# Transposing the adapter input by DMA instead of by TensorE and VectorE, in an attention kernel followed by a mixture of adapters

## The chip, the core and the metric

The kernel runs on one core of a Trainium2 chip. Five engines work side by side, each with its own instruction order: TensorE (PE in the profile, its weight loads PEld), VectorE (DVE), ScalarE (ACT), GpSimd (POOL) and SyncE (SP), which here only issues DMAs. An engine runs its instructions in the order in which the program gives them, and an instruction may wait for semaphores that other engines or DMAs raise. The metric is device time in microseconds of one execution, the median of several runs; the profile describes one further execution.

## The reference, cut to what matters

```python
scores = scale * q @ k.T + bias          # 8 batches, 8 heads, 576 positions, head size 64
attn   = softmax(scores) ; y = attn @ v  # bias from a table of 32 buckets, by distance
x = y.transpose(0, 2, 1, 3).reshape(8 * 576, 512)

logits = x @ w_gate                      # 8 adapters, the 2 best of each row
w = softmax(logits of the 2 best)
out = x + sum over them of w * ((x @ A[e]) @ B[e])   # A: 512 x 16, B: 16 x 512 each
```

Inputs and output are fp32; the kernel computes the matrix products in bf16.

## The kernel before

**Units and slots.** The attention is cut into 32 units: a unit `u` is one batch and one pair of heads (`hp`, 0 to 3), in the order `units` = (0,0), (0,1) ... (7,3). The main loop has six slots per unit. Each slot computes a part of the unit's scores on PE, exponentials on ACT (L260, L268), the bias products on DVE (L285, L274), and, for the unit before, the products with v (`values`, L303). In slot 5 `normalise` (L313, L314) writes the unit before into `xn`, the rows of x in bf16. A batch's rows are four tiles of 128 and 64 rows over; the spare rows of two batches share the tile `xe`, one half of which is moved by a DMA (L320).

**Loads.** `load(b)` makes a list of 28 DMAs for batch b, by head pairs: q, k and v of a pair (128 KB each head), with the last 64 positions after the first pair (`qke32`, `ve32`). The list is put on the SP queue, up to three DMAs a slot in units 0 and 1 and one or two later. Batch 0 and 1 are loaded at the start; batch b + 2 is put on the queue from slot 4 of the third unit of batch b. The staging buffers hold two batches. POOL casts q, k and v to bf16 two units and one unit ahead (`cast_qk`, `cast_v`, L129, L133), and the spare rows before the next batch (`cast_tails`). PE transposes q and k of a unit (`transpose_pe`, L224), DVE copies them out of PSUM (L228).

**SP's order.** All loads, the moves to `xe` and all stores of the output (L409) stand in one SP queue, in program order. A DMA there that has to wait holds up those behind it. The program uses eight completion semaphores for SP's DMAs in turn, so that each issue also waits for the eighth before it.

**Adapters.** A, w_gate and B are loaded by six DMAs of POOL in unit 3 (`load_adapters`, L204 to L209), which cast to bf16 on the way. Finished tiles of x are taken in groups of two or three by `Group`. Its steps: transposes of x on PE (`xT_pe`, L342) and the copy out of PSUM on DVE (`xT_out`, L347); the product with A and w_gate together (`zl_pe`, L355); the copy to SBUF on ACT (`z_copy`) and the choice of the two best (`gates`, DVE, POOL and ACT); the weights (`weigh`); the transpose of the weighted z (`zT_pe`, `zT_out`); and per tile the product with B (`dl_pe`, L403), the sum with x on DVE (`dl_out`, L407) and the store (L409). A step is a pair, a PE part and a DVE part. `batch_done` calls `enqueue`, one group after even batches and two after odd ones, and this puts the steps on a list, mixed with the last steps of the group before. `place` takes one step from the list in slots 0, 2 and 4 of a unit (in the last two batches in slot 5 too): the PE part goes into the next slot, the DVE part is done at the next `place`. The first group (three tiles of batch 0) has its `zl_pe` at the end of unit 5. The last batch's own rows are done by `Last` after the main loop, with transposes on PE; nothing in it changes.

Of the kernel before, what the change touches and what calls it, by code (L numbers as in the profile page):

```python
# [11 lines left out]
FP32 = mybir.dt.float32  # L12
BF16 = mybir.dt.bfloat16
# [20 lines left out]
def kernel(  # L34
# [34 lines left out]
    cp = ctx.enter_context(tc.tile_pool(name="const", bufs=1))  # L69
# [19 lines left out]
    def load(b):  # L89

        q32 = stg.tile([128, 4, H, D], FP32, name="q32", tag="q32")
        k32 = stg.tile([128, 4, H, D], FP32, name="k32", tag="k32")
        v32 = stg.tile([128, 4, H, D], FP32, name="v32", tag="v32")
        qke32 = stg.tile([128, H, D], FP32, name="qke32", tag="qke32")
        ve32 = stg.tile([128, HP, D], FP32, name="ve32", tag="ve32")
        staged[b] = (q32, k32, v32, qke32, ve32)
        todo = []

        def main(eng, t, src, hp):
            for h in (2 * hp, 2 * hp + 1):  # L100
                todo.append(lambda h=h: eng.dma_start(  # L101
                    out=t[:, :, h, :],
                    in_=src[b, h, :512, :].rearrange("(j p) d -> p j d", p=128)))

        for hp in range(HP):
            second = nc.scalar if b == 0 and hp == 0 else nc.sync
            main(nc.sync, q32, q, hp)
            main(second, k32, k, hp)
# [5 lines left out]
            main(nc.sync, v32, v, hp)  # L114
# [26 lines left out]
    units = [(b, hp) for b in range(B) for hp in range(HP)]  # L141
# [57 lines left out]
    AW = cp.tile([128, 4, ER + E], BF16, tag="AW")  # L199
    Bc = cp.tile([ER, Dm], BF16, tag="Bc")  # L200

    def load_adapters(c):
        if c < 4:
            nc.gpsimd.dma_start(out=AW[:, c, :ER].rearrange("p (e r) -> p e r", e=E),  # L204
                                in_=moe_A[:, c * 128:(c + 1) * 128, :].rearrange("e d r -> d e r"))
        elif c == 4:
            nc.gpsimd.dma_start(out=AW[:, :, ER:], in_=moe_w_gate.rearrange("(c p) e -> p c e", p=128))
        else:
            nc.gpsimd.dma_start(out=Bc, in_=moe_B.rearrange("e r d -> (e r) d"))  # L209


    xs, xe, probs, accs = {}, {}, {}, {}
# [94 lines left out]
    def normalise(u):  # L307
        b, hp = units[u]
        pv = accs.pop(u)
        if hp == 0:  # L310
            xs[b] = xp.tile([128, 5, Dm], BF16, name="xn", tag="xn")
        rc = ms.tile([128, 2, 5], FP32, name="rc", tag="rc")
        nc.vector.reciprocal(rc, _ap(pv, D, [[512, 2], [W, 5]]))  # L313
        nc.vector.tensor_tensor(  # L314
            _ap(xs[b], hp * 128, [[D, 2], [Dm, 5], [1, D]]),
            _ap(pv, 0, [[512, 2], [W, 5], [1, D]]),
            _ap(rc, 0, [[5, 2], [1, 5], [0, D]]), op=ALU.mult)
        if hp == HP - 1 and b % 2 == 0:
            xe[b // 2] = xp.tile([128, Dm], BF16, name="xe", tag="xe", bufs=2)
            nc.sync.dma_start(out=xe[b // 2][:64, :], in_=xs[b][64:, 4, :])  # L320
        if hp == HP - 1 and b % 2 and b + 1 < B:
            join(b, 0, Dm)

    def join(b, c0, c1):
        nc.vector.tensor_copy(xe[b // 2][64:, c0:c1], xs[b][64:, 4, c0:c1])


    queue = deque()
    state = {"now": None, "last": None}

    class Group:
# [3 lines left out]
            self.n = len(tiles)  # L335
            self.xT = []

        def xT_pe(self, t0, n):
            self.ps = mp.tile([128, n, 4, 128], BF16, name="xT_ps", tag="mm")
            for t in range(n):  # L340
                for c in range(4):
                    nc.tensor.transpose(self.ps[:, t, c, :],  # L342
                                        self.x[t0 + t][:, c * 128:(c + 1) * 128], ident)

        def xT_out(self, n):
            xT = ms.tile([128, n, 4, 128], BF16, name="xT", tag=f"xT{n}")
            nc.vector.tensor_copy(xT, self.ps)  # L347
            self.xT += [xT[:, t] for t in range(n)]

        def zl_pe(self, t0, n):  # L350
            if t0 == 0:
                self.zl = mp.tile([128, self.n, ER + E], FP32, name="zl", tag="mm")
            for t in range(t0, t0 + n):
                for c in range(4):
                    nc.tensor.matmul(self.zl[:, t, :], lhsT=self.xT[t][:, c, :], rhs=AW[:, c, :],  # L355
                                     start=(c == 0), stop=(c == 3), skip_group_check=True)
# [54 lines left out]
        def front(self):  # L411
            n2 = min(self.n, 2)
            s = [(lambda: self.xT_pe(0, n2), lambda: self.xT_out(n2))]
            if self.n == 3:
                s.append((lambda: self.xT_pe(2, 1), lambda: self.xT_out(1)))
                s.append((lambda: (self.zl_pe(0, 3), self.z_copy()), self.gates))
            else:
                s.append((lambda: (self.zl_pe(0, n2), self.z_copy()), self.gates))
            return s

        def middle(self):
            return [(self.zT_pe, self.zT_out)]

        def back(self):
            return [(lambda t=t: self.dl_pe(t), lambda t=t: self.dl_out(t))
                    for t in range(self.n)]
# [6 lines left out]
    def enqueue(tiles):  # L433
        gr, last = Group([tile_of(*t) for t in tiles]), state["last"]
        front, fill = gr.front(), last.back() if last else []
        fill += [(None, None)] * (2 - len(fill))
        pe, dve = fill[1]
        fill[1] = (pe, lambda: (dve and dve(), gr.weigh()))
        queue.extend(front[:1] + (last.middle() if last else []) + front[1:] + fill)
        state["last"] = gr  # L440

    def flush():
        if state["last"]:
            queue.extend(state["last"].middle() + state["last"].back())
            state["last"] = None

    due = {}

    def at(slot, fn, *args):
        due.setdefault(slot, []).append((fn, args))  # L450
# [16 lines left out]

    def batch_done(b):
        if b % 2 == 0:
            if b + 2 < B:  # L470
                enqueue([(b, 0), (b, 1), (b, 2)])
                left.append((b, 3))
            else:
                enqueue([(b, 0), (b, 1)])
                enqueue([(b, 2), (b, 3)])
# [105 lines left out]
    def finish(p, t):  # L581
        normalise(p)
        if units[p][1] == HP - 1:
            at(t + 1, batch_done, units[p][0])

    for t in range(SLOTS * NU):
        u, s = divmod(t, SLOTS)
        b, hp = units[u]
        p = u - 1
        scores(u, s)  # L590
        for fn, args in due.pop(t, []):
            fn(*args)
        if u == 3:
            load_adapters(s)
        for i in range(3 if u < 2 else 2 if s % 3 == 0 else 1):
            if loading:
                loading.popleft()()
        early = u >= NU - HP and hp in (0, HP - 1)
# [63 lines left out]
    u = NU - 1  # L662
# [6 lines left out]
    last = Last(B - 1)  # L669
# [43 lines left out]
```

## Time and profile before

| What | Value |
|---|---|
| median of 3 runs | 231.32 us (231.14 to 232.71) |
| the profiled execution | 233.92 us; its span, from the first to the last instruction, 231.8 us |
| TensorE clock granted, mean over the span | 0.955 |
| DMA moved | 39.74 MB in 126521 packets, 120464 of them under 512 bytes |
| the loads' queue | 68.2% of 16 engines' span; POOL's queue 3.5% |
| a load of 128 KB, from issue to landing | 2.9 to 3.1 us (median) |
| start of `xn` (L314) of units 3, 7, 15, 23, 31 | 41.09, 62.66, 114.77, 165.38, 216.99 us |

The busy share of an engine is the mean over stages with different limits. The chain of waits follows the execution back from its last instruction, at each step to what released it; a group row gives the operation, its tiles and shapes, the count, then the busy time in all and the mean of one in ns, and the idle time just before it with what ended it. A timeline row begins with start and duration in us; neighbouring instructions of one kind are merged, with their count at the end. In the timeline of SP a row is the issuing of DMAs, not their flight. A row of the table of stretches has the busy time of each engine in that stretch, with instructions in brackets, then the granted clock, the DMA engines' mean busy share (several queues can add up to more than 1) and GB/s.

### The profile page before, as it was taken

How to read it: one execution, taken by the hardware profiler on the slowest of the kernel's cores; microseconds unless marked ns; L12 is line 12 of the kernel's file. 1: busy time of each engine (PE TensorE's matmuls, PEld its weight loads, DVE VectorE, ACT ScalarE, POOL GpSimd, SP SyncE). 2: the span in 40 equal slices, each digit the busy share in tenths (PEclk: the TensorE clock that was granted, in tenths of full speed). 3: DMA queues.
4: the chain of work that ended last, by engine and by line, in shares of the span. 5: the costliest groups of instructions: out<-in, count | busy, mean ns of one | idle time of the engine just before them, and what ended most of it. 6: DMA issues, size and time to landing. Idle time of an engine off the chain costs nothing.

```text
span 231.8 us, 7224 instructions
## 1 busy us (share of the span) xinstructions
PE 181.6 (78%) x2900; PEld 121.7 (52%) x2900; DVE 174.9 (75%) x401; ACT 174.0 (75%) x225; POOL 97.1 (42%) x171
## 2 busy tenths in 40 slices
PE   0797857989899976888899976897888887796661
PEld 0354534666566663564566664565565655464530
DVE  5346763878798869787998869987988788987760
ACT  3587954999899876879789876897988767877422
POOL 2316497249413613805903613916507443411010
PEclk9999985999999999899999999999999999999955
DMA  7899899878879998797597785976597122222206
GB/s 163 199 244 221 188 161 208 186 165 202 196 170 234 223 247 203 208 246 184 137 229 185 210 201 146 251 172 173 114 230 214 48 77 73 90 48 95 90 29 199
DMA packets 126521, 39.74 MB, mean 171 GB/s; under 512 B 120464, under 2 KB 121880, under 8 KB 126488
## 3 DMA queue, kind: packets, MB, share of 16 engines
q1 hardware_dynamic: 120056, 38.62, 68.2%
q0 software_dynamic: 4832, 0.27, 3.5%
q10 hardware_dynamic: 1600, 0.40, 0.8%
q8 instruction: 22, 0.36, 0.6%
q14 instruction: 11, 0.09, 0.1%
HBM read 29.84 MB, written 9.45 MB: 169 GB/s over the span
## 4 chain that ended last, share of the span: by engine, by line
DVE 36%; PE 34%; ACT 8%; SPq 8%; issue 6%; DMA 4%; POOL 2%; POOLq 0%; ACTq 0%
DVE pm L285 12%; PE pv L303 11%; PE sc L256 9%; DVE xn L314 7%; ACT pm L260 7%; DVE ot L407 6%; SPq L101 5%; PE dl L403 2%; PE xT_ps L342 2%; DVE xT L347 2%; DVE rc L313 2%; PE tp L224 2%; PE zl L355 2%; DMA q<-in_q_dram 2%; DVE qkT L237 1%
## 5 line engine op out<-in xcount | busy, mean ns | idle before, releaser
L260 ACT ACTIVATE pm<-sc 128x1024 bf16<-128x1024 f32 (+1 forms) x160 | 142.2, 939 | 31.2 <-PE sc L256 30.2
L303 PE MATMUL pv<-vm,pm 128*128 128x65 bf16 x1280 | 63.0, 197 | 9.2 <-DVE xn L314 9.1
L285 DVE TENSOR_TENSOR pm<-pm,eb 128x512 bf16<-128x512 bf16 (+2 forms) x96 | 67.6, 725 | 2.4 <-DMA eb<-gx_d 1.9
L303 PEld LDWEIGHTS <-pm 128*128 128x128 bf16 x1280 | 51.2, 99 | 33.8 <-issue 20.7
L256 PE MATMUL sc<-qkT 64*128 64x384 bf16 (+7 forms) x512 | 61.9, 300 | 4.7 <-ACT pm L260 1.8
L370 POOL TENSOR_TENSOR ls<-z,top 128x24 f32<-128x24 f32 (+1 forms) x11 | 4.1, 372 | 66.1 <-DVE top L368 57.5
L256 PEld LDWEIGHTS <-qkT 64*128 64x128 bf16 x512 | 19.2, 95 | 20.8 <-issue 6.6
L224 PE MATMUL tp<-ident,qkn 128*128 128x128 bf16 x256 | 21.1, 227 | 10.5 <-DVE qkn L129 5.6
L228 DVE COPY qkT<-tp 128x1024 bf16<-128x1024 bf16 x32 | 21.9, 683 | 8.9 <-PE tp L224 8.9
L314 DVE TENSOR_TENSOR xn<-pv,rc 128x640 bf16<-128x640 f32 x32 | 26.4, 824 | 1.1
L133 POOL CAST vm<-v 128x512 bf16<-128x512 f32 x32 | 22.1, 690 | 10.3 <-DMA v<-in_v_dram 10.3
L129 POOL CAST qkn<-q 128x512 bf16<-128x512 f32 x30 | 23.1, 771 | 3.0 <-DMA q<-in_q_dram 1.5
L129 POOL CAST qkn<-k 128x512 bf16<-128x512 f32 x32 | 20.9, 652 | 6.6 <-DMA k<-in_k_dram 6.5
L268 ACT ACTIVATE pe<-sc 128x576 bf16<-128x576 f32 x32 | 20.8, 650 | 3.2 <-PE sc L266 2.2
L224 PEld LDWEIGHTS <-qkn 128*128 128x128 bf16 x256 | 15.9, 101 | 11.8 <-DVE qkn L129 5.6
L407 DVE TENSOR_TENSOR ot<-dl,xn 128x512 f32<-128x512 f32 x28 | 19.1, 683 | 2.8 <-PE dl L403 2.8
L266 PE MATMUL sc<-qkT 64*64 64x64 bf16 (+1 forms) x128 | 14.1, 294 | 7.5 <-ACT pm L260 7.3
L403 PE MATMUL dl<-Bc,zT 128*128 128x512 bf16 x31 | 12.2, 393 | 4.3 <-DVE ot L407 3.7
L313 DVE RECIPROCAL rc<-pv 128x10 f32<-128x10 f32 x32 | 6.9, 215 | 10.2 <-PE pv L303 10.2
L347 DVE COPY xT<-xT_ps 128x1024 bf16<-128x1024 bf16 (+1 forms) x20 | 11.2, 562 | 1.2 <-PE xT_ps L342 1.2
L266 PEld LDWEIGHTS <-qkT 64*64 64x64 bf16 x128 | 6.7, 105 | 9.3 <-issue 6.8
L385 POOL TENSOR_TENSOR gate<-nu,rd 128x24 f32<-128x24 f32 (+1 forms) x11 | 2.6, 239 | 19.4 <-DVE rd L383 8.7
(87 smaller groups left out, 164.8 us busy)
## 6 DMA issues: line engine op xcount, KB each, us to landing
q<-in_q_dram SPq DMA_DIRECT2D x64, 128.0 KB, 3.1
v<-in_v_dram SPq DMA_DIRECT2D x64, 128.0 KB, 2.9
k<-in_k_dram SPq DMA_DIRECT2D x62, 128.0 KB, 2.9
out_dram<-ot SPq DMA_DIRECT2D x28, 256.0 KB, 2.2
qke<-in_q_dram SPq DMA_DIRECT2D x8, 128.0 KB, 2.8
ve<-in_v_dram SPq DMA_DIRECT2D x16, 64.0 KB, 2.6
out_dram<-otL SPq DMA_DIRECT2D x4, 256.0 KB, 2.0
qke<-in_k_dram SPq DMA_DIRECT2D x7, 128.0 KB, 2.8
```

Of the source, the lines that this page charges most:

```text
L129: eng(out=nats[u][:, i].rearrange("p j (h d) -> p j h d", h=2), in_=src)
L133: eng(out=vals[b % 2][0][:, :, 2 * hp:2 * hp + 2, :D], in_=staged[b][2][:, :, 2 * hp:2 * hp + 2, :])
L224: nc.tensor.transpose(ps[:, i, j, :], nats[u][:, i, j, :], ident)
L228: nc.vector.tensor_copy(batch_tiles(b)[:, hp, :, :512], tps.pop(u).rearrange("p i j t -> p i (j t)"))
L256: nc.tensor.matmul(sc[:, h, c - SW * s:c - SW * s + w], lhsT=kT[rows, j * 128:(j + 1) * 128], rhs=qT[rows, q0:q0 + w], start=True, stop=True)
L260: nc.scalar.activation(pm[:, :, SW * s:end], sc[:, :, :n], ACT.Exp, scale=scale)
L266: nc.tensor.matmul(flat[rows, q0:q0 + n], lhsT=kT[rows, 512:], rhs=qT[rows, q0:q0 + n], start=True, stop=True)
L268: nc.scalar.activation(pe, flat[:, :S], ACT.Exp, scale=scale)
L285: nc.vector.tensor_tensor(t, t, e, op=ALU.mult)
L303: nc.tensor.matmul(pv[:, h, t * W:(t + 1) * W], lhsT=lhsT, rhs=rhs, start=(j == 0 and t == 0), stop=(j == 4), skip_group_check=True)
L314: nc.vector.tensor_tensor(_ap(xs[b], hp * 128, [[D, 2], [Dm, 5], [1, D]]), _ap(pv, 0, [[512, 2], [W, 5], [1, D]]), _ap(rc, 0, [[5, 2], [1, ...
L407: nc.vector.tensor_tensor(ot, self.dl, self.x[t], op=ALU.add)
```

## The change

Three things are changed.

1. x of a group is transposed by DMA, from SBUF to SBUF, one DMA of the SP queue per tile, issued all at once when the group is enqueued (`turn`). `xT_pe` and `xT_out` are gone. The list of steps is laid out anew, with pauses (steps that do nothing), so that the group's `zl_pe` comes four slots after the transposes are issued; for the last full batch (`tight`) without pauses. `batch_done` is called one slot later, and the DMA to `xe` is issued there.
2. A, w_gate and B are loaded in fp32 by six DMAs of the SP queue, put there in unit 2, between the loads of batch 1 and those of batch 2; three casts on POOL in slots 1, 3 and 5 of unit 4 make the bf16 tiles.
3. From batch 2 on a load takes 128 positions of all eight heads (256 KB): four each for q, k and v, first q and k in turn, then the spare rows of q and k, then v, then the spare rows of v: 16 DMAs a batch, one a slot.

In SP's order the transposes of the first group stand behind all loads of batch 2 and the move to `xe`, and ahead of the loads of batch 3.

```diff
+        def rows(t, src, j):
+            todo.append(lambda: nc.sync.dma_start(
+                out=t[:, j, :, :],
+                in_=src[b, :, j * 128:(j + 1) * 128, :].rearrange("h p d -> p h d")))
+
+        if b > 1:
+            for j in range(4):
+                rows(q32, q, j)
+                rows(k32, k, j)
...
     def load_adapters(c):
         if c < 4:
-            nc.gpsimd.dma_start(out=AW[:, c, :ER].rearrange("p (e r) -> p e r", e=E),
-                                in_=moe_A[:, c * 128:(c + 1) * 128, :].rearrange("e d r -> d e r"))
+            nc.sync.dma_start(out=Af[:, c, :].rearrange("p (e r) -> p e r", e=E),
+                              in_=moe_A[:, c * 128:(c + 1) * 128, :].rearrange("e d r -> d e r"))
...
+    def cast_adapters(i):
+        out, src = ((AW[:, :, :ER], Af), (AW[:, :, ER:], Gf), (Bc, Bf))[i]
+        nc.gpsimd.tensor_copy(out=out, in_=src)
...
             xe[b // 2] = xp.tile([128, Dm], BF16, name="xe", tag="xe", bufs=2)
-            nc.sync.dma_start(out=xe[b // 2][:64, :], in_=xs[b][64:, 4, :])
...
-        def xT_pe(self, t0, n):
-            self.ps = mp.tile([128, n, 4, 128], BF16, name="xT_ps", tag="mm")
-            for t in range(n):
-                for c in range(4):
-                    nc.tensor.transpose(self.ps[:, t, c, :],
-                                        self.x[t0 + t][:, c * 128:(c + 1) * 128], ident)
-
-        def xT_out(self, n):
-            xT = ms.tile([128, n, 4, 128], BF16, name="xT", tag=f"xT{n}")
-            nc.vector.tensor_copy(xT, self.ps)
-            self.xT += [xT[:, t] for t in range(n)]
...
+        def turn(self):
+
+            xT = ms.tile([128, self.n, 4, 128], BF16, name="xT", tag="xT", bufs=2)
+            for t in range(self.n):
+                nc.sync.dma_start_transpose(out=xT[:, t, :, :], in_=self.x[t])
+            self.xT = [xT[:, t] for t in range(self.n)]
...
+    def enqueue(tiles, tight=False):
         gr, last = Group([tile_of(*t) for t in tiles]), state["last"]
...
+        gr.turn()
+        gate, weigh, zT, first, *rest = gr.steps()
+        old = (last or []) + [pause] * (2 - len(last or []))
+        new = [pause, gate, old[0], weigh, old[1], pause, zT, first]
+        queue.extend(x for x in new if not (tight and x is pause))
+        state["last"] = rest
...
     def batch_done(b):
         if b % 2 == 0:
+            nc.sync.dma_start(out=xe[b // 2][:64, :], in_=xs[b][64:, 4, :])
...
-            at(t + 1, batch_done, units[p][0])
+            at(t + 2, batch_done, units[p][0])
...
-        if u == 3:
+        if u == 2:
             load_adapters(s)
-        for i in range(3 if u < 2 else 2 if s % 3 == 0 else 1):
+        if u == 4 and s % 2:
+            cast_adapters(s // 2)
+        for i in range(3 if u < 2 else 2 if s % 3 == 0 and b == 0 else 1):
```

More of the change, by code (lines that the diff above doesn't have):

```diff
@@ L103, in main @@
                     in_=src[b, h, :512, :].rearrange("(j p) d -> p j d", p=128)))
-        for hp in range(HP):
+        def rows(t, src, j):
[6 more added lines that the diff above has]
+                rows(k32, k, j)
+        for hp in range(HP if b < 2 else 1):
             second = nc.scalar if b == 0 and hp == 0 else nc.sync
-            main(nc.sync, q32, q, hp)
-            main(second, k32, k, hp)
+            if b < 2:
+                main(nc.sync, q32, q, hp)
+                main(second, k32, k, hp)
             if hp == 0:
@@ L113, in load @@
                         in_=src[b, :, 512:, :].rearrange("h p d -> p h d")))
-            main(nc.sync, v32, v, hp)
+            if b < 2:
+                main(nc.sync, v32, v, hp)
+            else:
+                for j in range(4):
+                    rows(v32, v, j)
             if hp == 0:
@@ L200 @@
     Bc = cp.tile([ER, Dm], BF16, tag="Bc")
+    Af = cp.tile([128, 4, ER], FP32, tag="Af")
+    Gf = cp.tile([128, 4, E], FP32, tag="Gf")
+    Bf = cp.tile([ER, Dm], FP32, tag="Bf")
     def load_adapters(c):
         if c < 4:
-            nc.gpsimd.dma_start(out=AW[:, c, :ER].rearrange("p (e r) -> p e r", e=E),
-                                in_=moe_A[:, c * 128:(c + 1) * 128, :].rearrange("e d r -> d e r"))
+            nc.sync.dma_start(out=Af[:, c, :].rearrange("p (e r) -> p e r", e=E),
+                              in_=moe_A[:, c * 128:(c + 1) * 128, :].rearrange("e d r -> d e r"))
         elif c == 4:
-            nc.gpsimd.dma_start(out=AW[:, :, ER:], in_=moe_w_gate.rearrange("(c p) e -> p c e", p=128))
+            nc.sync.dma_start(out=Gf, in_=moe_w_gate.rearrange("(c p) e -> p c e", p=128))
         else:
-            nc.gpsimd.dma_start(out=Bc, in_=moe_B.rearrange("e r d -> (e r) d"))
+            nc.sync.dma_start(out=Bf, in_=moe_B.rearrange("e r d -> (e r) d"))
+    def cast_adapters(i):
+        out, src = ((AW[:, :, :ER], Af), (AW[:, :, ER:], Gf), (Bc, Bf))[i]
+        nc.gpsimd.tensor_copy(out=out, in_=src)
     xs, xe, probs, accs = {}, {}, {}, {}
@@ L336, in __init__, with zl_pe @@
             self.xT = []
-        def xT_pe(self, t0, n):
-            self.ps = mp.tile([128, n, 4, 128], BF16, name="xT_ps", tag="mm")
-            for t in range(n):
-                for c in range(4):
-                    nc.tensor.transpose(self.ps[:, t, c, :],
-                                        self.x[t0 + t][:, c * 128:(c + 1) * 128], ident)
-        def xT_out(self, n):
-            xT = ms.tile([128, n, 4, 128], BF16, name="xT", tag=f"xT{n}")
-            nc.vector.tensor_copy(xT, self.ps)
-            self.xT += [xT[:, t] for t in range(n)]
[L350 to L353, printed above, removed]
+        def turn(self):
[3 more added lines that the diff above has]
+            self.xT = [xT[:, t] for t in range(self.n)]
+        def zl_pe(self):
+            self.zl = mp.tile([128, self.n, ER + E], FP32, name="zl", tag="mm")
+            for t in range(self.n):
                 for c in range(4):
@@ L409, in dl_out, with steps @@
                 nc.sync.dma_start(out=out[n0:n0 + cnt, :], in_=ot[p0:p0 + cnt, :])
[L411 to L426, printed above, removed]
+        def steps(self):
+            return ([(lambda: (self.zl_pe(), self.z_copy()), self.gates), (None, self.weigh),
+                     (self.zT_pe, self.zT_out)]
+                    + [(lambda t=t: self.dl_pe(t), lambda t=t: self.dl_out(t))
+                       for t in range(self.n)])
     def tile_of(b, t):
@@ L431, in tile_of @@
         return xe[b // 2], [(64 * o, (b - 1 + o) * S + 512, 64) for o in range(2)]
-    def enqueue(tiles):
+    pause = (None, None)
+    def enqueue(tiles, tight=False):
         gr, last = Group([tile_of(*t) for t in tiles]), state["last"]
[L435 to L440, printed above, removed]
+        gr.turn()
[4 more added lines that the diff above has]
+        state["last"] = rest
     def flush():
-        if state["last"]:
-            queue.extend(state["last"].middle() + state["last"].back())
-            state["last"] = None
+        queue.extend(state["last"] or [])
+        state["last"] = None
     due = {}
@@ L473, in batch_done @@
             else:
-                enqueue([(b, 0), (b, 1)])
-                enqueue([(b, 2), (b, 3)])
+                enqueue([(b, 0), (b, 1)], True)
+                enqueue([(b, 2), (b, 3)], True)
                 flush()
```

## The prediction

> **What bounds the kernel now.** I read the page's busy line and its chain first, then the groups by shape, then the timelines of the SP queue, POOL and PE for the first 65 us, and the table of stretches for the clock and the DMA rate.
>
> ```profile
> PE 181.6 (78%) x2900; PEld 121.7 (52%) x2900; DVE 174.9 (75%) x401; ACT 174.0 (75%) x225; POOL 97.1 (42%) x171
> ...
> DVE pm L285 12%; PE pv L303 11%; PE sc L256 9%; DVE xn L314 7%; ACT pm L260 7%; DVE ot L407 6%; SPq L101 5%; PE dl L403 2%; PE xT_ps L342 2%; DVE xT L347 2%; DVE rc L313 2%; PE tp L224 2%; PE zl L355 2%; DMA q<-in_q_dram 2%; DVE qkT L237 1%
> ```
>
> Three engines are near 75% and the chain changes between them: a late, balanced stage. Only the start differs, where SPq L101 (the load issues) is in the chain.
>
> ```profile
> L342 PE MATMUL xT_ps<-ident,xn 128*128 128x128 bf16 x112 | 9.2, 220 | 0.3 <-DVE ot L407 0.3
> ...
> L347 DVE COPY xT<-xT_ps 128x1024 bf16<-128x1024 bf16 x11 | 7.5, 679 | 0.0
> ...
> L347 DVE COPY xT<-xT_ps 128x512 bf16<-128x512 bf16 x9 | 3.8, 420 | 1.2 <-PE xT_ps L342 1.2
> ```
>
> These are the rows that go. The next fence holds SP's issues at the start, then PE.
>
> ```profile
> 26.88 1.33 SPq L101 DMA_DIRECT2D q<-in_q_dram  x2
> ...
> 40.98 0.99 SPq L101 DMA_DIRECT2D q<-in_q_dram  x2
> ...
> 59.99 1.05 SPq L101 DMA_DIRECT2D v<-in_v_dram  x2
> ```
> ```profile
> 42.29 0.61 PE L224 MATMUL tp<-ident,qkn 128*128 128x128 bf16 x8
> ...
> 46.80 0.88 PE L355 MATMUL zl<-AW,xT 128*128 128x136 bf16 x12
> ```
>
> To be seen: SP issues without pause. At 26.88 head pair 1 of batch 1 begins, at 40.98 batch 2, and at 59.99 stands the last pair of batch 2. PE does the first group's zl at 46.80, in unit 5, when 8 of batch 2's 28 loads have been issued. So up to some 60 us the loads run hardly ahead of the work; later nothing waits for them for long.
>
> **Removed: x's transposes.** 31 tiles lose 4 transposes each; eight take 0.61 us in the PE timeline, 0.077 each, so 0.31 us of PE per tile. DVE loses 7.5 + 3.8 = 11.3 us, 0.365 per tile. What it is worth: from the xn of unit 7 to that of unit 15 (62.66 to 114.77, eight units, nine tiles) 52.1 us pass. DVE's rows make 4.3 us per unit and 1.42 per tile, 47.4 in all; ACT's make 5.35 per unit (4 x 1.022 + 0.608 + 0.650), and 0.72 for each of three groups, 45.0. Without L347 DVE has 44.1. DVE alone could give 3.3 us per eight units, PE 9 x 0.31 = 2.8, and ACT next in line keeps some of it: I take 2.3. The first group's three tiles lie before 46.8, which leaves 28: 28/9 x 2.3 = **-7 us** (bounds -3, and -10, all of DVE's 28 x 0.365).
>
> **Added: the wait of the first group.** SP's order in the built program decides here. In the changed kernel the SP queue holds, one behind the other: the rest of batch 1's loads, six adapter loads, all 16 loads of batch 2 (twelve of 256 KB, two of 128, two of 64), xe, then the three transposes of the first group. The third carries a wait for the second v block of batch 2 (SP reuses eight completion semaphores, so each issue waits for the eighth before it). zl stands in PE's order where it stood, at the end of unit 5, and now needs these three. Behind it on PE stand scores and values of everything, and ACT and DVE wait for these. So zl moves from 46.8 to the landing of the transposes:
>
> - Batch 1's last loads: 18 issues run from 26.88 to batch 2's start. They took 14.0 us, during which the rate sagged and POOL's own adapter DMAs ran; the ten before took 6.0, 0.60 each. Without that contention 18 x 0.60 ends at 37.7; with it 40.9. I take 38.
>
> ```profile
> 20.00:24.00 4.00, 3.33 (x65) 2.13 (x66) 3.83 (x6) 3.46 (x5) 3.36 (x5) 1.00 1.02 231
> ...
> 34.00:36.00 2.00, 0.60 (x4) 0.34 (x4) 0.46 (x2) 0.00 (x0) 2.00 (x3) 0.50 2.01 209
> ```
>
> (Columns at the end: granted clock, DMA share, GB/s.) The loads alone reach 231 GB/s at a share of 1.02: that is full.
>
> - Adapters in fp32: 0.53 MB in pieces of 64 bytes mostly. At 203 GB/s (the mean of 8 to 41 us) 2.6 us; POOL's queue used 24.3% of those 33 us for as many packets, 8.0. I take 4, nearer to the bytes.
> - Batch 2: 3.54 MB at 225 GB/s, 15.7 us (13.6 at 260, the best 7 us stretch; 17.4 at 203). The rows moved to token tiles keep the bytes and the 256-byte pieces; 28 issues become 16.
> - Three transposes of 128 KB. No such row exists. From below, bytes alone at 225: 0.58 each, 1.7. From above, each like a lone xe, 2.2 from issue to landing: 6.6. I take 2.0, as the queue is kept full, and one landing of 2.2:
>
> ```profile
> L320 SPq DMA_DIRECT2D xe<-xn x4: 488/514/525, 52.9 to 192.4; - x4
> ...
> DMA to landing us min/median/max: 2.0/2.2/3.2
> ```
>
> Sum 38 + 4 + 15.7 + 2.0 + 2.2 = 61.9, so zl is late by **+15.1 us** (bounds: 37.7 + 2.6 + 13.6 + 1.7 + 2.0 = 57.6, +10.8; 40.9 + 8.0 + 17.4 + 6.6 + 2.2 = 75.1, +28). Nothing gives this back: the loads are then far ahead, but before has no starved PE after 46.8 to be relieved.
>
> A rule against the change stands on the Trainium skill's page "VectorE: DVE Perf Modes", section "The three transpose paths": TensorE 390 ns for a 128x128, the crossbar DMA 1309 ns, so TensorE where PSUM will do. Four of these in series per tile would make 5.2 us and the end some 14 us later than mine. "DMA: Bandwidth & Descriptors", section "Latency and other measured facts", has 261 GB/s for such a transpose, an estimate of 0.5 us per tile. TensorE's row here is 220 ns and 77 pipelined, better than the page; no run shows the DMA's.
>
> **The later groups' wait.** After odd batches two groups are queued at once, and zl of the first comes four slots later. In unit 5 the time from the end of xn (41.92) to zl (46.80) is 4.9 us. Three issues of 0.5 and 2.2 to landing make 3.7: covered. With 2.2 each it is 8.8, and 3.9 us are lost three times, 11.7. I take **+1**. The groups of even batches have four entries ahead of them in the list of steps, and slack.
>
> **POOL.** Six DMA issues go, 5.0 us (L204, L207, L209: 3.7 + 0.8 + 0.5), four of them among the casts that PE waited for until 36.19:
>
> ```profile
> 34.76 0.76 POOL L207 DMA_DIRECT2D AW<-in_moe_w_gate_dram  x1
> 35.50 0.63 POOL L129 CAST qkn<-k 128x512 bf16<-128x512 f32 x1
> ```
>
> That is worth up to 2 us at unit 4. In their place three casts come in unit 4, the first ahead of casts for unit 6, and it waits for A's fourth load, some 42 us; then tp of unit 6 is at 45 instead of 42.29, -2 to +2.7. Both are over before 61.9, so the wait at zl covers them: 0. Without that cover they are the whole change of the start.
>
> **Small terms.** PE idles for about 15 us. In the stretch above, after a pause, the granted clock was 0.50, and it stayed there to 40; ten pv matmuls took 0.73 us instead of 0.48. One more such spell: **+1**. The list of steps has 8 entries per group where it had 7 and runs one entry past the main loop (an ot of 0.68): **+0.7**. xe is issued later, by tiles that need it last: 0, hidden by the next group's slack; its 2.2 us if that goes.
>
> **Sum.** +15.1 - 7 + 1 + 1 + 0.7 = +10.8. The profiled execution took 233.92 us (span 231.8) and would take 244.7; it is 1.1% above the median of the runs, 231.32, so by the ratio 1.046 I predict **242**.
>
> **Rivals.**
> - *The wait is not there* (faster): the gain alone, 231.3 - 7 + 1.7, 226. It decides if zl runs before about 51 us (4.3 us late, what is left of the gain). For it: DMA share has room on average (74%). Against it: 28 + 6 + 16 loads stand ahead on SP, and 3.54 MB from 42 to 49 would be 500 GB/s. Chance 0.07.
> - *A short wait and the whole gain*: +10.8 - 10 + 1.7, 234; a shade better is no change. For it: the 260 GB/s stretch. Chance 0.13.
> - *Transposes are dear*: 2.2 us each in the queue. 4.6 more at the start and 11.7 - 1 more for the later groups: 242 + 15, 257. For it: SP's issues are single and in order, and no row bounds them. Chance 0.17.
> - *ACT keeps the gain*: the late stage doesn't shrink by more than 3 us, 246; it lies within the forecast's own spread (237 to 249). Forecast with this: 0.63.
>
> **Numbers.** The range takes in the short wait and most of the dear transposes: 230 to 255. A measurement of this kernel can tell about 1% from no change. Faster by more: 0.07, the first rival; within 1%: 0.07, half of the second; slower: 0.86.
>
> **What will show it.** In the changed profile: PE idle some 15 us at zl in unit 5, ended by the xT DMA, and SP's transposes issued at 55 to 60; a page without xT copies, xn to xn over eight units near 50 us instead of 52; the stretch after the pause at a clock of 0.5. The prediction is wrong if zl comes before 52 us (then SP did not hold the transposes), if transposes take over 2 us each, or if later zl's wait.

## The result, and the profile after

The changed kernel takes **267.71 us** (median of 4 runs, 265.98 to 269.34) against 231.9 for the kernel before: ratio **1.154** (95% interval 1.146 to 1.163), 15% slower. The direction was forecast, the size was not: 242 was the forecast and 255 the upper end of the range. The profiled execution took 269.34 us, its span is 267.6. Ratios here and below leave out executions over 1.5% longer than the fastest of their kernel, while the medians keep them, so the two can differ a little.

The first fence holds three lines of the page of the changed kernel: the busy line, and the chain by engine and by line.

```profile
PE 188.6 (70%) x2776; PEld 121.9 (46%) x2776; DVE 165.8 (62%) x381; ACT 173.8 (65%) x225; POOL 93.8 (35%) x168
...
PE 28%; SPq 23%; DVE 19%; DMA 14%; ACT 8%; issue 4%; POOL 2%; POOLq 0%; ACTq 0%
PE pv L325 10%; SPq L101 9%; PE sc L278 8%; DMA xT<-xn 7%; ACT pm L282 6%; SPq L106 6%; DVE pm L307 5%; DVE xn L336 5%; PE tp L246 3%; DMA v<-in_v_dram 3%; SPq L363 3%; PE dl L418 2%; PE zl L370 2%; DVE ot L422 2%; DMA out_dram<-ot 2%
```

DVE lost 9 us of work, as intended, and no engine is at 75% any more. In the chain stand names that were not there: `SPq L106` and `SPq L363` (the later loads and the transposes being issued), `DMA xT<-xn`, `DMA v<-in_v_dram`. SP and the DMAs now make 37% of it.

Where the time went is read from the start of `xn` of single units (positive: lost against the kernel before):

| Stretch | before | after | lost |
|---|---|---|---|
| to xn of unit 3 | 41.09 | 40.24 | -0.9 |
| units 4 to 7 | 21.57 | 44.56 | **+23.0** |
| units 8 to 15 | 52.11 | 51.76 | -0.4 |
| units 16 to 23 | 50.61 | 55.33 | +4.7 |
| units 24 to 31 | 51.61 | 61.48 | **+9.9** |
| the rest of the span | 14.8 | 14.2 | -0.6 |

**The first group.** SP's issues from 40 to 67 us, then PE:

```profile
40.18 4.28 SPq L222 DMA_DIRECT2D Af<-in_moe_A_dram  x4
...
45.73 0.37 SPq L106 DMA_DIRECT2D q<-in_q_dram  x1
...
60.38 1.77 SPq L131 DMA_DIRECT2D ve<-in_v_dram  x2
62.25 0.56 SPq L476 DMA_DIRECT2D xe<-xn  x1
62.85 3.92 SPq L363 DMA_TRANSPOSE xT<-xn  x3
```
```profile
65.50 0.64 PE L370 MATMUL zl<-AW,xT 128*128 128x136 bf16 x4 [11.05 <-DMA xT<-xn]
66.65 0.64 PE L370 MATMUL zl<-AW,xT 128*128 128x136 bf16 x4 [0.51 <-DMA xT<-xn]
67.92 0.64 PE L370 MATMUL zl<-AW,xT 128*128 128x136 bf16 x4 [0.64 <-DMA xT<-xn]
```

The adapters stand where the forecast put them, and so do the loads of batch 2; the transposes are issued last, and the matmuls of each tile wait for their own one. The table of stretches (columns as before: PE, PEld, DVE, ACT, POOL, then clock, DMA share, GB/s) shows the core standing still meanwhile, with a DMA share over 1, and the half clock after it:

```profile
56.00:64.00 8.00, 0.00 (x0) 0.00 (x0) 0.22 (x1) 0.00 (x0) 0.00 (x0) 0.63 1.22 210
64.00:68.00 4.00, 1.35 (x9) 0.80 (x10) 0.00 (x0) 0.00 (x0) 0.00 (x0) 0.50 0.47 102
68.00:72.00 4.00, 4.00 (x42) 2.52 (x42) 2.01 (x8) 2.44 (x4) 1.98 (x5) 0.54 1.15 224
```

**The later groups.** Units 9, 17 and 25 took 11.31, 13.21 and 13.64 us, where the kernel before took 6.01, 6.02 and 6.94. These are the units after odd batches. SP ahead of unit 17:

```profile
139.23 2.19 SPq L424 DMA_DIRECT2D out_dram<-ot  x2
141.52 3.14 SPq L106 DMA_DIRECT2D v<-in_v_dram  x4
144.76 7.01 SPq L363 DMA_TRANSPOSE xT<-xn  x5
```

Unit 15's `xn` began at 136.56 and was done at 137.4, but the transposes were issued only from 144.76 on, 7.4 us later, behind stores and loads of v. Ahead of unit 25 it was 8.3 us, ahead of unit 9 only 2.2, and there the slow issues weigh more: five took 8.19 us of SP. And the transposes themselves, in the view of the tile xT (count, then ns of the shortest, the median and the longest issue; start of the first and the last):

```profile
L363 SPq DMA_TRANSPOSE xT<-xn x28: 1199/1257/2959, 62.9 to 233.0; - x28
...
DMA to landing us min/median/max: 2.3/2.4/4.2
```

One is 1.26 us of SP's time, where a load of 128 KB or a move to `xe` is 0.5 to 0.6, and lands 2.4 us after its start. Of the waits that grew, those of POOL, DVE and ACT for the choice of the two best follow from zl; behind them stands PE's wait for xT:

```profile
PE zl L370 <- DMA xT<-xn: 27.0, 10, 11.1
```

12.2 us of this are the first group's, and 13.5 belong to units 9, 17 and 25, which are together 19.2 us longer than before. Each later wait, too, was followed by a low clock: 0.52 from 92 to 96 us, 0.50 from 148 to 152, 0.60 from 204 to 208. How much of the other 5.7 us this makes was not measured.

### The profile page after: what moved, and what is told of

Read it like the earlier page. It is cut to its first block, busy times and chain, and to the rows that moved or that the text cites. A ratio compares the mean times of both kernels' runs of the same rounds, so it can differ in the third digit from the quotient of the medians.

```text
span 267.6 us, 6885 instructions
## 1 busy us (share of the span) xinstructions
PE 188.6 (70%) x2776; PEld 121.9 (46%) x2776; DVE 165.8 (62%) x381; ACT 173.8 (65%) x225; POOL 93.8 (35%) x168
## 4 chain that ended last, share of the span: by engine, by line
PE 28%; SPq 23%; DVE 19%; DMA 14%; ACT 8%; issue 4%; POOL 2%; POOLq 0%; ACTq 0%
PE pv L325 10%; SPq L101 9%; PE sc L278 8%; DMA xT<-xn 7%; ACT pm L282 6%; SPq L106 6%; DVE pm L307 5%; DVE xn L336 5%; PE tp L246 3%; DMA v<-in_v_dram 3%; SPq L363 3%; PE dl L418 2%; PE zl L370 2%; DVE ot L422 2%; DMA out_dram<-ot 2%
## 5 line engine op out<-in xcount | busy, mean ns | idle before, releaser
L325 PE MATMUL pv<-vm,pm 128*128 128x65 bf16 x1280 | 67.0, 203 | 6.2 <-DVE xn L336 6.0
L325 PEld LDWEIGHTS <-pm 128*128 128x128 bf16 x1280 | 53.8, 103 | 33.4 <-issue 19.1
L278 PE MATMUL sc<-qkT 64*128 64x384 bf16 (+7 forms) x512 | 65.0, 313 | 5.7 <-ACT pm L282 3.0
L246 PE MATMUL tp<-ident,qkn 128*128 128x128 bf16 x256 | 23.7, 244 | 13.5 <-POOL qkn L143 7.2
L370 PE MATMUL zl<-AW,xT 128*128 128x136 bf16 x124 | 13.1, 259 | 27.0 <-DMA xT<-xn 27.0
L278 PEld LDWEIGHTS <-qkT 64*128 64x128 bf16 x512 | 20.0, 96 | 23.5 <-issue 10.8
L143 POOL CAST qkn<-k 128x512 bf16<-128x512 f32 x32 | 23.6, 736 | 8.1 <-DMA k<-in_k_dram 8.1
L383 DVE MAX8 top<-z 128x8 f32<-128x8 f32 x31 | 3.2, 158 | 37.2 <-ACT z L375 37.2
L375 ACT COPY z<-zl 128x408 f32<-128x408 f32 (+1 forms) x11 | 5.3, 481 | 31.1 <-PE zl L370 31.1
L246 PEld LDWEIGHTS <-qkn 128*128 128x128 bf16 x256 | 17.8, 110 | 14.7 <-POOL qkn L143 7.9
L370 PEld LDWEIGHTS <-xT 128*128 128x128 bf16 x124 | 8.8, 111 | 31.9 <-DMA xT<-xn 30.3
```

The lines of the kernel that those rows point to most:

```text
L143: eng(out=nats[u][:, i].rearrange("p j (h d) -> p j h d", h=2), in_=src)
L246: nc.tensor.transpose(ps[:, i, j, :], nats[u][:, i, j, :], ident)
L278: nc.tensor.matmul(sc[:, h, c - SW * s:c - SW * s + w], lhsT=kT[rows, j * 128:(j + 1) * 128], rhs=qT[rows, q0:q0 + w], start=True, stop=True)
L325: nc.tensor.matmul(pv[:, h, t * W:(t + 1) * W], lhsT=lhsT, rhs=rhs, start=(j == 0 and t == 0), stop=(j == 4), skip_group_check=True)
```

## The experiments

They are ordered by question, not by date; each expectation stands as written before its run. Ratios are to the kernel before, measured beside it. One point of a ratio is 2.3 us.

### The other two parts and the list of steps

**e9_steps**: the changed kernel with its new list of steps and the call one slot later, but transposes on TensorE, loads by head pairs, adapters by POOL.

```diff
-        gr.turn()
...
-        new = [pause, gate, old[0], weigh, old[1], pause, zT, first]
+        if pe:
+            two = min(gr.n, 2)
+            new = [(lambda: gr.xT_pe(0, two), lambda: gr.xT_out(0, two))]
+            if gr.n == 3:
+                new.append((lambda: gr.xT_pe(2, 1), lambda: gr.xT_out(2, 1)))
+            new += [gate, old[0], weigh, old[1], zT, first]
```

> Only the new list of steps is left of the change: all groups transpose on PE (in the place of the list's two pauses), loads by head pairs, adapters by POOL, as before. Theory list: the longer units 24, 26 and 31 of the run with all groups on PE (7.6 us together) belong to the list, where zT and the product behind it stand in neighbouring slots once four steps are placed per unit; the start is as before: 235 to 239. Rival, the loads by token tiles lengthen the end: as before, 229 to 233.

Measured: 240.78 us, 1.032 (1.027 to 1.037), a little above the range expected. The list alone costs 3.2 points, 7 us. This is a balance: units 8 to 15 took 48.8 us instead of 52.1, units 24 to 31 took 59.7 instead of 51.6, above all units 24 and 31 with 8.9 and 9.9 us (before: 5.3 and 5.1). In the last two batches a step is placed in slots 0, 2, 4 and 5 of a unit, so that some steps come in neighbouring slots, and the new list has `zT` and the first `dl` side by side, where the old one had the next group's steps between them. So `dl` waits for its zT to be copied (PE timeline of this kernel, idle time and its releaser in brackets):

```profile
166.13 0.34 PE L417 MATMUL zT_ps<-ident,zt 128*128 128x128 bf16 x3 [0.26 <-POOL zt L410]
168.93 0.39 PE L426 MATMUL dl<-Bc,zT 128*128 128x512 bf16 x1 [2.14 <-DVE zT L422]
```

In the kernel before the same `dl` at 174.20 waits for nothing. What else of units 24 to 31 the list costs was not taken apart.

**e10_rows**: e9_steps with the later loads by token tiles.

> As the run with only the new list of steps, plus the loads by token tiles from batch 2 on; adapters still by POOL. Theory: the adapters on SP cost most of the 11 us that the run with all groups on PE had lost by unit 7, and the token tiles the 3 us after unit 5 (the casts of the spare rows of v wait for the last load): 2 to 4 us more than with the list alone, 238 to 243. Rival, the token tiles cost nothing and it was all the adapters: within 1 us of the list alone.

Measured: 244.8 us, 1.053 (1.048 to 1.057), a little above the range expected and 2.1 points (5 us) more than e9_steps (the two profiled executions differ by only 1.1 us in span). Unit 6 took 9.68 us instead of 6.19: POOL's cast of q waits, for in the order of the loads the first pair of batch 2 has all its q and k only after eight of the 256 KB loads.

```profile
POOL qkn L143 <- DMA q<-in_q_dram: 6.6, 1, 6.6
```

(Waits from 50 to 64 us of this kernel: total, times, longest.)

**e1_pe_all**: the changed kernel with all transposes on TensorE, so e10_rows with the adapters on SP.

> All groups transpose x on PE again, with the copy on DVE, in the changed kernel's list of steps (the two transposing steps take the place of its two pauses); loads by token tiles and adapters on the SP queue stay as changed. Theory SP order (zl waits for transposes that stand behind loads on SP): no wait of PE at zl is left; the POOL wait for the adapters stays, so unit 4 ends about 7.7 us later than before and the rest runs as before, 238 to 242. Rival, the loads by token tiles are what starves the late units: the long units 9, 17 and 25 stay at 11 to 13 us and the time stays above 255. Rival, the step list gives the shorter units seen between the waits (5.6 us less over eight units): then 8 to 15 us less than 240.

Measured: 249.0 us, 1.069 (1.062 to 1.077), missed: it lies between the expectation and its first rival, since the list and the loads had been held to be free. Units 9, 17 and 25 took 6.0, 6.0 and 6.7 us, so the loads do not make the long units. The adapters on SP cost 1.7 points, 4 us. The DMA transposes, taken by themselves, so cost 1.154 - 1.069 = 8.5 points, 20 us of 36 (8.0 points with the loads and adapters of before, e5_pairs against e9_steps). The rest comes from what the forecast held to be small.

### The wait of the first group

**e2_pe_first**: the changed kernel with the first group's transposes on TensorE.

```diff
-                enqueue([(b, 0), (b, 1), (b, 2)])
+                enqueue([(b, 0), (b, 1), (b, 2)], pe=b == 0)
```

> Only the first group (three tiles of batch 0) transposes on PE; all else as in the changed kernel. Theory SP order: of the 22 us lost by unit 5, the 14 after unit 4 go (zl waited from 54.5 to 67.9), the adapter wait of POOL stays, and the three later long units stay: 252 to 256. Rival, the start is lost to the adapters and the load rate whatever the transposes do: 262 to 268.

Measured: 257.97 us, 1.102 (1.093 to 1.111), 2 us above the range expected and 5.2 points (12 us) less than the changed kernel: that is the first group's wait. Units 9, 17 and 25 still took 12.4, 12.6 and 13.4 us.

**e3_adapters_pool**: the changed kernel with the adapters loaded by POOL as before.

> The adapters are loaded by POOL's DMAs with the cast on the way, in unit 3, as before; all else as in the changed kernel. Theory SP order: POOL's 11 us wait goes and unit 4 is some 7 us shorter, but zl of the first group still waits for SP, which only saves its six adapter issues (5.5 us): 261 to 264, with the wait at zl longer than now. Rival, the adapter wait is a cost of its own on top: about 8 us and more come back, 256 to 260.

Measured: 258.32 us, 1.106 (1.099 to 1.113). zl of the three tiles starts at 58.69 to 61.37, some 6.6 us earlier: the six DMAs that stood on SP in front of it had taken 5.55 us there, where the forecast had 4. The total is in the rival's range. Unit 4 fell from 13.89 to 4.90 us, as both had it; but unit 5 took 21.04 us, and PE still waited 11.8 us for xT in one piece, which is the theory's mechanism. By unit 7 this kernel is 6.6 us ahead of the changed one; the other 6.4 us come after it, with units 17 and 25 at 10.3 and 11.1 us, where nothing of the adapters stands. This was not explained. Moving the adapters is worth 4.9 points here and 1.7 where TensorE transposes: the parts do not add up freely.

**e4_copy**: a plain copy of the same bytes in place of each transposing DMA. The transposition is left out, so the adapters' part is computed from x in the wrong layout; the rest is the same.

```diff
-                nc.sync.dma_start_transpose(out=xT[:, t, :, :], in_=self.x[t])
+                nc.sync.dma_start(out=xT[:, t, :, :], in_=self.x[t].rearrange("p (c k) -> p c k", c=4))
```

> The DMAs that transpose become plain copies of the same 128 KB from SBUF to SBUF at the same place of the SP queue; x is not transposed, so the adapters' part of the output is not the reference's. Theory SP order: the place in the queue is what counts; an issue costs about 0.5 instead of 1.25 us, so each of the four waits of PE at zl is 2 to 3 us shorter and no more: 256 to 262. Rival, the transposing itself is dear (engine time, or holding up the queue): the waits nearly go, 235 to 250.

Measured: 257.03 us, 1.098 (1.089 to 1.108). A copy takes 0.55 to 0.6 us of SP instead of 1.26, and the waits remain: 18.73 us in unit 5, and 10.7, 9.3 and 11.2 in units 9, 17 and 25. Over the kernel before these four units are 25.3 us longer, with transposing DMAs 33.4. So most of the waits belongs to the DMAs' place in the queue; but in the total, transposing instead of copying is 5.6 of the 8.5 points, the larger part.

**e8_act**: all transposes issued by ACT.

```diff
-                nc.sync.dma_start_transpose(out=xT[:, t, :, :], in_=self.x[t])
+                nc.scalar.dma_start_transpose(out=xT[:, t, :, :], in_=self.x[t])
```

> All transposes are issued from ACT's queue instead of SP's, at the same place of the program; else as the changed kernel. No load or store stands ahead of them there, but each issue takes ACT's time (1.25 us on SP, 39 us for 31). Theory SP order: zl's waits go nearly (under 3 us each), the first group's zl comes before 55 us although batch 2's loads are not done, and ACT, with 174 + 39 us busy, sets the time: 245 to 262, the waits of PE for the transposes under a third of the 27 us before. Rival, the transposes wait for the DMA engines, which are the same for both queues: zl still comes after 60 us, and the time stays above 262.

Measured: 275.04 us, 1.185 (1.178 to 1.191); missed in the total, and by 1 us in the time of zl. The first group's zl ran at 56.2 to 58.7 instead of 65.5 to 68.6, so SP's order did hold it. But the waits moved into ACT, whose exponentials now stand behind its DMA issues:

```profile
ACT pm L282 <- DMA xT<-xn: 18.6, 4, 7.1
ACT pm L282 <- DMA v<-in_v_dram: 14.6, 2, 7.6
```

The second row is a load of SP's queue: in this program ACT's issues take their completion semaphores from the same eight as SP's, so an issue on ACT waits for loads of SP.

### The waits of the later groups

**e5_pairs**: DMA transposes and the new list, but loads by pairs and adapters by POOL.

> The first part of the change alone: x transposed by DMA with the new list of steps; loads by head pairs (28 issues of 128 KB a batch, at the rate of before) and adapters by POOL in unit 3, as before. Theory SP order: 19 of batch 2's 28 loads stand ahead of the first group's transposes, some 10 us of loads like the 16 larger ones, so zl of the first group comes near 58 to 60 us as it did with the adapters on POOL, and the three later waits stay: 252 to 262. Rival, the loads by token tiles make the waits: 235 to 245.

Measured: 258.72 us, 1.112 (1.104 to 1.120); units 5, 9, 17 and 25 took 17.7, 10.3, 12.5 and 14.4 us. The waits come with the DMA transposes also where loads and adapters are as before.

**e6_loads2**: the changed kernel with two loads per slot, so that SP has a batch's loads behind it before the transposes.

```diff
-        for i in range(3 if u < 2 else 2 if s % 3 == 0 and b == 0 else 1):
+        for i in range(3 if u < 2 else 2):
```

> From unit 2 on two loads per slot instead of one, so that a batch's v blocks stand in SP's order well ahead of the next transposes and of more stores; else as the changed kernel. Theory SP order: the first wait stays (the same loads stand ahead), the three later long units lose 3 to 5 us each: 253 to 260. Rival, the transposes' own time makes the later waits: they stay, 265 to 269.

Measured: 264.06 us, 1.134 (1.127 to 1.142); missed. Unit 9 took 5.74 us, so its wait went. Units 17 and 25 kept theirs (13.4 and 14.0). For unit 17 loads of v and stores of the output still stood ahead: its rows were complete at 131.4 us, and the transposes were issued from 138.69 on:

```profile
135.19 2.11 SPq L131 DMA_DIRECT2D ve<-in_v_dram  x2
137.39 1.20 SPq L424 DMA_DIRECT2D out_dram<-ot  x2
138.69 6.48 SPq L363 DMA_TRANSPOSE xT<-xn  x5
```

**e7_pe_odd1**: e2_pe_first, and the first group after odd batches on TensorE too; 19 tiles stay with DMA.

> The first group and the first group after each odd batch (the four whose zl waited) transpose on PE, the others by DMA; else as the changed kernel. Theory SP order: no long unit is left but that of the adapters' wait, and 19 of 31 tiles still leave DVE: 5 to 12 us below the run with all groups on PE (249), so 237 to 244. Rival, the waits move to the next groups (their transposes stand behind the same loads and stores): 248 to 256.

Measured: 241.11 us, 1.035 (1.028 to 1.043). Of PE's waits for transposing DMAs this is left, for its weight loads (its matmuls wait 0.9 us in all):

```profile
PEld L386 <- DMA xT<-xn: 1.3, 2, 1.1
```

From e2_pe_first to here the time falls by 6.7 points, 15.5 us: the wait of the later groups, less what nine tiles gain by DMA. From e1_pe_all to here, where only 19 tiles change from TensorE to DMA, it falls by 3.4 points, 7.9 us or 0.41 us per tile: the gain is there, where nothing waits for it. (For the last two groups the list without pauses is here one step shorter each than in e1_pe_all; e13_slack11 has the gain without that difference.)

### DMA transposes alone, in the kernel before

If that is right, the kernel before should gain from DMA transposes placed where zl comes late enough. These four change nothing else: list, loads and adapters are those of the kernel before.

**e11_slack**: 17 late tiles by DMA: the groups of batches 2 and 4, the second group after batches 1, 3 and 5, and the last group.

```diff
-    def front(self):
+    def front(self, dma):
+            if dma:
+                self.turn()
+                gate = (lambda: (self.zl_pe(0, self.n), self.z_copy()), self.gates)
+                return [(None, None)] * (self.n - 1) + [gate]
...
-                enqueue([(b, 0), (b, 1), (b, 2)])
+                enqueue([(b, 0), (b, 1), (b, 2)], b > 0)
...
-                enqueue([(b, 2), (b, 3)])
+                enqueue([(b, 2), (b, 3)], True)
...
-            enqueue([(b, 2), (b, 3), (b, 4)])
+            enqueue([(b, 2), (b, 3), (b, 4)], True)
```

> The kernel before, its list of steps, loads and adapters, with x transposed by DMA only in the groups whose zl comes late anyway: after even batches from 2 on, the second group after odd batches, and the second of the last two; 17 of 31 tiles. Theory SP order: no zl waits, DVE and PE are relieved of 0.365 and 0.31 us per tile: 4 to 7 us faster, 225 to 229. Rival, SP or the DMA engines have no room for 17 issues of 1.25 us in the middle stage, and loads come late: 232 or more.

Measured: 234.89 us, 1.002 (0.998 to 1.006); missed, with the total in the rival's range. The start of unit 21's xn was 4.4 us ahead of the kernel before (148.38 against 152.73), then unit 22 took 14.42 us instead of 7.26. SP, then PE:

```profile
147.01 1.68 SPq L101 DMA_DIRECT2D q<-in_q_dram  x1
148.79 0.52 SPq L320 DMA_DIRECT2D xe<-xn  x1
149.41 3.83 SPq L341 DMA_TRANSPOSE xTd<-xn  x3
```
```profile
151.90 0.48 PE L361 MATMUL zl<-AW,xTd 128*128 128x136 bf16 x4 [2.90 <-DMA xTd<-xn]
```

The rows of batch 4 were complete at 137.9 (xn of unit 19: 137.04 + 0.82), but their move to `xe` came at 148.79: **SP was 10.9 us behind**. In the kernel before the same move followed its rows at once (DVE, then SP):

```profile
140.02 0.82 DVE L314 TENSOR_TENSOR xn<-pv,rc 128x640 bf16<-128x640 f32 x1
```
```profile
140.91 0.53 SPq L320 DMA_DIRECT2D xe<-xn  x1
```

So the transposes themselves put SP behind: from 104 to 152 us its issues fill 44.7 of 48 us, in the kernel before 38.2. PE's waits for xTd make 4.4 us of the 7.2 that unit 22 is longer; the granted clock was 0.53 from 152 to 154 us and 0.50 to 158.

**e12_slack14**: e11_slack with the group of batch 4 back on TensorE.

```diff
-                enqueue([(b, 0), (b, 1), (b, 2)], b > 0)
+                enqueue([(b, 0), (b, 1), (b, 2)], b not in (0, 4))
```

> This is the kernel before with the DMA transposes for 14 late tiles only: as e11_slack, but the group of batch 4 goes back to TensorE and VectorE. In e11_slack the SP queue issued for 7.5 to 8.1 of every 8 us from 64 to 152 us (before: 5.0 to 7.5 from 104 to 152 us), the move to xe of batch 4 came at 148.79 us, 10.9 us after its rows (137.04 + 0.83), and zl waited in unit 22, which took 14.42 us. Theory (SP's time for issuing is the resource that gives out, each transpose takes 1.25 us of it): without those three transposes no unit is longer than before by 2 us; unit 21 stays about 3 to 4 us ahead of the kernel before, and the gain is kept to unit 31: 226 to 230 us, ratio 0.975 to 0.99. Rival (the transposes cost elsewhere what they give, by contention or by the clock, and the stall in unit 22 was only where it showed): a stall of several us comes in another unit, and the total stays at 232 to 236 us.

Measured: 231.55 us, 0.990 (0.984 to 0.995), between the two ranges expected. Unit 22 took 7.27 us, but in this profile unit 14 took 11.69: the group of batch 2, the other one of an even batch, whose move to `xe` was issued at 95.36, 8.6 us after its rows.

**e13_slack11**: no group of an even batch by DMA; 11 tiles are left.

```diff
-                enqueue([(b, 0), (b, 1), (b, 2)], b > 0)
+                enqueue([(b, 0), (b, 1), (b, 2)], b == 6)
```

(In this branch b is 0, 2 or 4, so the condition is never true.)

> The kernel before with DMA transposes for 11 tiles: the second group after each of batches 1, 3 and 5, and the second of the last two groups; no group of an even batch. In e11_slack (17 tiles) unit 22 took 14.42 us, in e12_slack14 (14 tiles, without the group of batch 4) unit 14 took 11.69 us, each time the zl of the group of an even batch, whose move to xe and transposes stand on the SP queue 9 to 11 us after their rows. Theory (what counts is where the group's place on the SP queue lies against its zl): no unit over 9 us after unit 3, PE waits under 1 us for xTd, and the gain is 11 tiles times 0.41 us (the rate of e1 against e7), 4.5 us: 226 to 230 us, ratio 0.975 to 0.99. Rival (the transposes use up a rate, of the SP queue or of the DMA engines, that is gone wherever they are put): a stall moves once more, to another unit, and the total is 231 to 235 us.

Measured: **226.81 us, 0.975 (0.971 to 0.979)**, 2.5% faster than the kernel before: as the theory said. After unit 3 no unit took over 7.3 us, and among the waits none for xTd is left that shows. The view of the tile xTd:

```profile
L341 SPq DMA_TRANSPOSE xTd<-xn x8: 1223/1254/1539, 70.7 to 188.5; - x8
...
  ACT z L366: 0.2, 1
...
DMA to landing us min/median/max: 2.4/3.4/4.3
```

(The second line is who waited for it, us and times.) SP issues for 44.5 of the 48 us from 104 to 152, hardly less than in e11_slack, its moves to `xe` of batches 2 and 4 are still 8.1 and 7.2 us behind their rows, and a transpose lands in 3.4 us (median; 2.5 there). What differs is that zl of a second odd group stands behind all the steps of the first, later than SP's lag: the transposes were all issued by 75.6, 123.5, 173.1 and 189.8 us, their zl came at 84.2, 133.4, 179.6 and 199.7. By the medians the gain over the kernel before beside it is 6.0 us, 0.55 us per tile.

**e14_late_zl**: e11_slack with all 17 tiles at their places on SP, but zl of batches 2 and 4 three steps later in PE's order.

```diff
-                return [(None, None)] * (self.n - 1) + [gate]
+                return [(None, None)] * (self.n - 2 + dma) + [gate]
...
-                enqueue([(b, 0), (b, 1), (b, 2)], b > 0)
+                enqueue([(b, 0), (b, 1), (b, 2)], (b > 0) + 3 * (b in (2, 4)))
```

> As e11_slack, with all its 17 DMA transposes at the same places on the SP queue, but the zl of the groups of batches 2 and 4 stands three steps (six slots, about 6 us) later in PE's order. Theory (a late place on the queue costs only where zl stands too early): the stalls of units 14 and 22 go although not one DMA is taken away; no unit over 9 us after unit 3; gain 17 times 0.41 us, 7 us: 223 to 228 us, ratio 0.96 to 0.98. Rival (SP's time for issuing or the DMA rate is used up): the loads come late instead, POOL's casts or zl wait for DMAs for several us in some unit, and the total stays at 231 to 236 us.

Measured: 234.37 us, 1.001 (0.997 to 1.005): half of each. The stalls of units 14 and 22 are gone (5.59 and 5.68 us), without a DMA less, and at unit 22 the kernel was 8.8 us ahead (151.15 against 159.99). Then units 23 to 28 lost 11 us. Waits from 165 to 202 us:

```profile
ACT pm L260 <- PE sc L256: 9.7, 5, 3.2
DVE ot L413 <- DMA out_dram<-ot: 7.3, 3, 3.9
```

DVE waits for stores: five of them were issued only from 187.29 on, behind loads, a wait that the kernel before does not have in that stretch. The later zl also pushes all steps behind it towards the last batches. Which of the two costs more stays open: no run has one without the other.

## Why the prediction was right and wrong

The terms of its sum, and what the runs showed in their place (differences of ratios, each good to about 1 point, 2 us):

| Term | predicted | measured | from |
|---|---|---|---|
| first group's wait, adapters on SP and the half clock | +15.1 + 1 | +12.0 + 3.9 | changed - e2; e1 - e10 |
| gain | -7 | -7.9 | e7 - e1, 19 tiles |
| later groups' wait | +1 | **+15.5** | e2 - e7 |
| list of steps | +0.7 | **+7.4** | e9 - before |
| loads by token tiles | 0 | **+4.8** | e10 - e9 |
| sum | +10.8 | +35.7 | |

The measured terms are steps of one chain of runs, so that they add up to the whole by construction. In another order they are different (the adapters were worth 4.9 points in e3_adapters_pool), and "later groups' wait" is net of what nine tiles gain by DMA.

**The start was right as a mechanism; that its weight on the total came out (15.9 against 16.1) is partly luck.** By its own steps zl was too early by 6 us: batch 1's loads ended at 40.2 (38 forecast), the adapters took 5.55 us of SP (4), batch 2 to the move to `xe` 16.5 (15.7), that move 0.6 (forgotten), three transposes 3.9 (2.0); the last landing was 1.1 shorter than the 2.2 added. All but the move and the landing lay inside the bounds given. The total does not show these 6 us, because other delays already lay under the wait, the cover that the prediction spoke of: without zl's wait, in e1_pe_all and e2_pe_first, unit 4 took 12.5 to 13 us all the same, since POOL's cast of the adapters waits for A and the casts that PE needs stand behind it (waits of e1_pe_all from 38 to 60 us):

```profile
POOL AW L231 <- DMA Af<-in_moe_A_dram: 10.6, 1, 10.6
...
PE tp L246 <- POOL qkn L143: 5.0, 1, 5.0
```

The prediction named that ("without that cover they are the whole change of the start") and costed it at -2 to +2.7; by unit 7 e1_pe_all was 11.0 us late, of which the list and the loads account for 5.1 (e10_rows), so that some 5.9 are left for the adapters. The half clock, counted once, came after each wait of PE.

**The step that failed: "The later groups' wait. [...] I take +1".** It took SP to be free when xn is done, and counted three issues and a landing from there. SP was not free: stores and the v rows of the next batch stood in front (144.76 against 137.4), and the term measured **+15.5** (e2_pe_first against e7_pe_odd1). The upper bound, 11.7, was for the price of transposes alone and left the queue out, so it was too low as well. The dear issue (1.26 us against the 0.5 of the `xe` row) comes on top. The rival of dear transposes had the nearest figure, 257, but for 2.2 us each, which no run shows; and with copies in place of transposes 12.2 of the 19.2 us by which units 9, 17 and 25 had grown remain (e4_copy).

**The small terms that were not small.** The list of steps was costed by its length, one entry at 0.68, and not by which steps became neighbours; it is +7.4. The moved loads were costed by bytes and pieces, which stay, and not by when the first pair of a batch is complete; that is +4.8 (e10_rows). The prediction's own sign of failure, "if later zl's wait", is what the profile shows.

**The gain was there**, and larger than assumed: 0.41 us per tile in e7_pe_odd1 and 0.55 in e13_slack11 against 0.25. That -7.9 stands beside -7 is luck, for it comes from 19 tiles instead of 28.

## What to carry to other kernels

Before work is moved from an engine to a DMA, read how far the queue that will issue it lags, and how much room it has for the new issues. Here the lag is the time from the end of xn to the issue of the `xe` move behind it. In the kernel before it was 11.0, 2.4, 0.1 and 0.1 us for batches 0, 2, 4 and 6: large at the start, and gone in the middle, where it would have misled. With 17 tiles moved (e11_slack) it was 9.0, 7.6, 10.9 and 0.0, since each transpose takes 1.26 us of a queue that was issuing for 38 of the 48 us from 104 to 152 already. What is needed sooner than the lag after the change stays on the engine, what is needed later goes (e13_slack11: 11 tiles, 2.5% faster; all 31 with the rest of the change: 15% slower). And the parts that come along with a change deserve a row each: who stands next to whom in the new order, and when the first consumer has all of its data.

## What the runs showed of the hardware

- A DMA transpose of a 128x512 bf16 tile from SBUF to SBUF holds the SP queue for 1.26 us (a copy of the same bytes 0.55 to 0.6) and lands after 2.4 us in the changed kernel (medians; 3.4 in e13_slack11, 3.5 in e8_act). In e8_act, where the transposes have ACT's queue nearly to themselves, it used 9.1% of 16 engines over 274.4 us, 25.0 us; less the 2 us of that queue's other work this is 0.74 us of all engines per tile.
- The Trainium skill's page "VectorE: DVE Perf Modes", section "The three transpose paths", has 1309 ns for a 128x128 by DMA; four in series would be an estimate of 5.2 us per tile, and 2.4 us from issue to landing was measured, so that this price cannot be taken four times here.
- The granted clock was 0.63 over the pause from 56 to 64 us, 0.50 from 64 to 68, where PE worked a third of the time, 0.54 from 68 to 72, where it was busy throughout, and 1.00 from 72 to 76: it came back later than the work.
- Four loads of A, 64 KB each, in pieces of 64 bytes, took 4.28 us of SP; the two loads of 128 KB just before them took 1.05 together.
- With adapters on SP, unit 0's xn starts at 22.0 to 22.4 us, with POOL's adapters at 19.7 to 20.5; by unit 3 it is made up. This was not explained.
